# Attention and feed-forward kernel: zero matmuls counted at their cold length, and new instruction lists

## The chip, the cores and the metric

One NeuronCore of a Trainium2 chip runs the whole program. The metric is the device time of one execution in microseconds. Lower is better.

## The reference

The inputs are q, k and v of shape (8, 8, 576, 64) (batch, heads, sequence, head size) and four weight matrices; all are float32. Attention works inside chunks of 64 positions, nine to a batch entry:

```python
scores = scale * np.matmul(q_c, k_c.transpose(0, 1, 2, 4, 3))   # by chunk, scale = 1/8
scores = scores - np.max(scores, axis=-1, keepdims=True)
attn = np.exp(scores)
attn = attn / (np.sum(attn, axis=-1, keepdims=True) + 1e-09)
out = np.matmul(attn, v_c)
...
x = out.transpose(0, 2, 1, 3).reshape(4608, 512)                # heads side by side
a = x @ w1          # 512 -> 1024
b = x @ w2          # 512 -> 1024
h = a * b @ w3      # 1024 -> 1024
return h @ w_out    # 1024 -> 512, float32
```

## The kernel before

The 4608 rows are 36 groups of 128 (two chunks, eight heads). Four groups make a tile of 512 rows for the feed-forward part, so there are nine tiles. All matmuls are in bfloat16 and sum into PSUM in float32.

A group g runs through these steps; the name of each is what the lists use:

- `qk{g}.0`, `qk{g}.1`: loads of q and k, with a cast, issued by GpSimd (POOL) into `raw`. A group whose two chunks lie in two batch entries has four.
- `t{g}`: 16 or 8 transposes on TensorE into the PSUM tile `p_tr`, of which there is one. Then `kc{g}` copies k to `kT`, and `q{g}.0` and `q{g}.1` copy the two halves of q into a block diagonal tile `qd`. Each copy is on ScalarE (ACT) or VectorE (DVE). For the groups that have a `tq{g}` in SyncE's (SP) list, the transposition is a DMA into `kqT` instead, and there is no `kc`.
- `s{g}`: eight score matmuls into `p_sc`, of which there is one. `mx{g}` takes the maxima. Then `sd{g}` (subtraction, VectorE) and one wide `ex{g}` (exponential, ScalarE), or, for the groups in `EXP_8`, an `ex{g}` of eight instructions, one by head, straight from `p_sc` with no `sd`.
- `sm{g}`: sums and reciprocals. `an{g}`: the division, on VectorE or GpSimd.
- `at{g}` (four transposes on TensorE) and `ac{g}` (copy), or `ta{g}` (a DMA on SyncE's queue).
- `av{g}`: eight matmuls with v into `p_av`, and `x{g}`, the copy into the tile's x.

The weights w3 and w_out are multiplied first, by `wt` (eight transposes of a block of w3), `wc` (copy), `wm` (matmuls in four parts, `wm{block}.{part}`) and `wr` (copy). The product is `w3o`. The first two blocks of w3 come over SyncE's queue in float32 (`f0`, `f1`) and are cast by `cast0` and `cast1`. Then a tile i takes, for each of eight column blocks j, `a{i}.{j}` and `b{i}.{j}` (four matmuls each), `c{i}.{j}` (ScalarE copies a out of PSUM) and `m{i}.{j}` (VectorE multiplies it by b); and for each of four row groups `o{row}` (eight matmuls with `w3o`), `y{row}` (copy) and `z{row}` (store, SyncE). The loads `w12.{j}.{n}` bring w1 and w2 for columns j and j+1; `v{b}.{n}` bring v. `zv` and `zq` zero the tiles of v and q, `ident` makes the identity for the transposes.

Nothing is ordered at run time. `ORDER` holds one list of step names for each engine, and each engine runs its list in order: an instruction whose operands are not there holds up all behind it on its engine. `Plan.run` walks through these lists with a cost for each step. From that come the order in which the program is recorded, which buffers a step takes, and a planned start of each step. At most eight loads are under way from each of the two issuing queues.

Ahead of steps in the first 20 us of the plan, the program puts matmuls of zeros on TensorE (`fill`, line 556, tile `cold` into the PSUM tile `p_av`): so many as fit, by a formula, between the end of TensorE's step before and the planned start of the step. Line 648 gives the number:

```python
if o.engine == "PE" and o.start < WARM:
    n = int((o.start - idle_from - (2.6 if idle_from < 2 else 0.5)) / 0.217)
```

`idle_from` is 1.2 before the first step. The program built so has 26 zero matmuls: four ahead of `wt0`, ten ahead of `t0`, four ahead of `s0`, five ahead of `t2` and three ahead of `s2`.

Line numbers in the profile: 318 and 321 loads of q and k, 330 of v, 338 of w1 and w2, 347 of w3, 370 of w_out; 356 the float32 rows of w3; 392 and 397 `t`; 401 `tq`, 407 `ta`; 434 `s`; 442 `mx`; 446 `sd`; 449 and 454 `ex`; 458 and 460 `sm`; 464 `an`; 469 `at`; 480 `av`; 527 `wt`; 538 `wm`; 556 the zero matmuls; 571 `a` and `b`; 580 `m`; 600 `o`; 618 `z`; 267, 269, 271 and 273 the helper that makes all copies; 282 `zv`; 286 `zq`.

Of the kernel before, what the change touches and what calls it, by code (L numbers as in the profile page):

```python
# [22 lines left out]
WARM = 20  # L23
ORDER = {
# [14 lines left out]
           "o30 b8.4 a8.4 b8.3 a8.3 b8.5 o31 o32 o33 o34 o35a o35b ").split(),  # L39
    "ACT":  # L40
# [9 lines left out]
           "c8.0 c8.2 c8.1 c8.7 c8.6 y29 c8.5 y30 c8.4 c8.3 y35b ").split(),  # L50
    "DVE":
# [11 lines left out]
           "y25 m7.0 m7.4 m7.3 y26 x32 m7.6 m7.2 m7.1 m8.0 m8.2 m8.1 y28 m8.7 m8.6 m8.4 m8.5 m8.3 y31 y32 y33 y34 y35a ").split(),  # L63
    "POOL":
# [8 lines left out]
           "an34 an35 ").split(),  # L73
# [4 lines left out]
           "z32 z30 z33 z34 z35a z35b ").split(),  # L78
}
PACKED = (0, 1, 2, 3, 4, 5, 6, 7, 8, 9, 11, 14, 15, 16, 18, 20, 26, 28, 29, 35)  # L80
EXP_8 = (2, 9, 13, 14, 15, 31, 32)
TURN_QK = [f"tq{g}" in ORDER["SP"] for g in range(36)]
TURN_A = [f"ta{g}" in ORDER["SP"] for g in range(36)]
ROWS_F32 = sum(t[0] == "f" for t in ORDER["SP"])
# [107 lines left out]
def kernel(  # L192
# [51 lines left out]
    ident = consts.tile([P, P], bf)  # L244
# [30 lines left out]
    cold = consts.tile([P, TT], bf, name="cold")  # L275
# [30 lines left out]
    def load_qk(g):  # L306
        (b0, c0), (b1, c1) = chunks(g)
        parts = [(slice(0, P), b0, c0, 2)] if b0 == b1 else [(halves[0], b0, c0, 1), (halves[1], b1, c1, 1)]
        box = raws[g] = {"ops": []}
        packed = g in PACKED and not TURN_QK[g]  # L310
        for w, src in enumerate((q, k)):
# [65 lines left out]
    def add_group(g):  # L377
# [4 lines left out]

        turned, packed, by_head = TURN_QK[g], g in PACKED, g in EXP_8

# [262 lines left out]
    with tc.manual_schedule():  # L647
        order, spells, idle_from = plan.run(), {}, 1.2
        for o in order:
            if o.engine == "PE" and o.start < WARM:  # L650
                n = int((o.start - idle_from - (2.6 if idle_from < 2 else 0.5)) / 0.217)
                if n > 0:
                    spells[o] = n
                idle_from = o.start + o.cost
        filler = fill(spells)
        for o in order:
            for _ in range(spells.get(o, 0)):
                next(filler)
            o.emit(o.engine)
# [30 lines left out]
```

## Time and profile before

| What | us |
|---|---|
| Median of three runs | 258.38 (258.14 to 259.05) |
| The profiled execution | 258.92 |
| Its span, first to last instruction | 257.1 |
| TensorE (PE) busy | 243.6 |
| VectorE (DVE) busy | 171.5 |
| ScalarE (ACT) busy | 140.0 |
| GpSimd (POOL) busy, issuing loads included | 117.7 |

The profile is of one execution. PE is TensorE's matmuls and PEld its weight loads, which run beside them. A matmul's duration holds its drain, which overlaps the next one; how long a row of matmuls holds TensorE is read from the start of the row to the start of the next. A wait is put down to what came last by the profile.

### The profile page before, as it was taken

The page shows a single profiled execution, that of the slowest core. Times are in us where ns is not written, and L with a number is a line of the kernel's source. Part 1 is how long each engine was busy: PE and PEld are TensorE (multiplying, and loading weights), DVE is VectorE, ACT ScalarE, POOL GpSimd, SP SyncE. Part 2 cuts the span into 40 slices and gives each one's busy share as a digit, 9 for nine tenths or more (in the row PEclk, how much of TensorE's full clock was granted, in tenths as well). Part 3 has the DMA queues.
Part 4 walks back from the last instruction along what each step waited for, and adds up shares of the span by engine and source line. Part 5 has one row for each costly group of instructions (what it writes and reads, how often), then busy time and mean ns, then how long its engine had stood idle before and what let it go on. Part 6 is the DMA issues. An engine that isn't in the chain of part 4 may idle for free.

```text
span 257.1 us, 4876 instructions
## 1 busy us (share of the span) xinstructions
PE 243.6 (95%) x1850; PEld 124.1 (48%) x1850; DVE 171.5 (67%) x315; ACT 140.0 (54%) x276; POOL 117.7 (46%) x146
## 2 busy tenths in 40 slices
PE   4879999999999989999989999989999999999994
PEld 2345555555545444554544445435444544544443
DVE  3168989975599765899696368988757585332342
ACT  5449887657476658445783645453684532432200
POOL 8777558979858656088408111763131031000000
PEclk9999999999999999999999999999999999999999
DMA  8999999999999999999999938699999239400334
GB/s 200 184 197 199 169 148 147 169 167 117 133 155 157 156 157 156 157 148 150 128 146 146 115 65 162 65 144 126 220 268 253 53 116 307 174 3 0 122 119 167
DMA packets 148999, 38.33 MB, mean 149 GB/s; under 512 B 138096, under 2 KB 143472, under 8 KB 148976
## 3 DMA queue, kind: packets, MB, share of 16 engines
q0 software_dynamic: 108192, 18.88, 99.3%
q1 hardware_dynamic: 40784, 19.14, 38.4%
q8 instruction: 14, 0.23, 0.4%
q14 instruction: 9, 0.07, 0.1%
HBM read 38.80 MB, written 9.44 MB: 188 GB/s over the span
## 4 chain that ended last, share of the span: by engine, by line
PE 72%; DVE 16%; ACT 5%; DMA 5%; issue 1%; DVEq 0%; ACTq 0%
PE ffn L571 41%; PE ffn L600 17%; DMA at<-an 3%; DVE ss L458 3%; DVE qd L273 3%; PE ffn L538 3%; PE p_av L480 3%; PE p_sc L434 2%; PE p_tr L392 2%; DVE abT L580 2%; DVE nm L442 2%; PE p_av L556 2%; DVE an L464 2%; DMA stage<-in_moe_w_dram 1%; DVE sd L446 1%
## 5 line engine op out<-in xcount | busy, mean ns | idle before, releaser
L571 PE MATMUL ffn<-xt,w_sb 128*128 128x512 bf16 x576 | 135.5, 379 | 0.0
L571 PEld LDWEIGHTS <-w_sb 128*128 128x128 bf16 x576 | 53.1, 98 | 56.3
L600 PE MATMUL ffn<-w3o_sb,abT 128*128 128x512 bf16 (+1 forms) x296 | 67.2, 373 | 0.0
L271 ACT COPY a_sb<-ffn 128x512 f32<-128x512 f32 x72 | 41.4, 591 | 47.1 <-PE ffn L571 46.9
L580 DVE TENSOR_TENSOR abT<-a_sb,ffn 128x512 bf16<-128x512 f32 x72 | 47.8, 678 | 27.7 <-PE ffn L571 15.1
L464 POOL TENSOR_TENSOR an<-e,rs 128x512 bf16<-128x512 bf16 x18 | 18.9, 1049 | 79.3 <-DVE rs L460 56.9
L600 PEld LDWEIGHTS <-abT 128*128 128x128 bf16 x296 | 28.2, 98 | 30.6
L442 DVE TENSOR_REDUCE nm<-p_sc 128x8 f32<-128x512 f32 x36 | 24.5, 681 | 15.2 <-PE p_sc L434 15.1
L449 ACT ACTIVATE e<-sd 128x512 bf16<-128x512 f32 x29 | 18.3, 633 | 19.1 <-DVE sd L446 18.5
L458 DVE TENSOR_REDUCE ss<-e 128x8 f32<-128x528 bf16 x36 | 24.9, 693 | 5.0 <-ACT e L454 2.5
L318 POOL DMA_DIRECT2D raw<-in_k_dram x29 | 24.9, 867 | 4.6 <-DMA raw<-in_q_dram 2.2
L318 POOL DMA_DIRECT2D raw<-in_q_dram x29 | 25.0, 874 | 3.2 <-DMA raw<-in_k_dram 1.8
L271 ACT CAST xt<-p_av 128x512 bf16<-128x512 f32 x27 | 15.8, 586 | 16.0 <-PE p_av L480 15.8
L446 DVE TENSOR_TENSOR sd<-p_sc,nm 128x512 f32<-128x512 f32 x29 | 19.8, 683 | 0.4
L330 POOL DMA_DIRECT2D vd<-in_v_dram x16 | 18.8, 1175 | 1.5 <-DMA raw<-in_k_dram 1.0
L434 PEld LDWEIGHTS <-qd 128*128 128x128 bf16 x288 | 12.4, 98 | 12.9 <-ACT qd L271 3.4
L538 PE MATMUL ffn<-wo_sb,w3t 128*128 128x512 bf16 x64 | 17.0, 380 | 0.2 <-DVE w3t L273 0.2
L480 PEld LDWEIGHTS <-vd 128*128 128x128 bf16 x288 | 12.9, 98 | 8.1 <-DMA at<-an 1.2
L273 DVE COPY o_sb<-ffn 128x512 f32<-128x512 f32 (+1 forms) x12 | 8.0, 666 | 11.1 <-PE ffn L600 11.1
L480 PE MATMUL p_av<-at,vd 128*128 128x64 bf16 x288 | 14.3, 193 | 0.7 <-DMA at<-an 0.7
L454 ACT ACTIVATE e<-p_sc,nm 128x64 bf16<-128x64 f32 x56 | 12.3, 337 | 4.7 <-DVE nm L442 4.7
L271 ACT COPY o_sb<-ffn 128x512 f32<-128x512 f32 (+1 forms) x13 | 7.4, 572 | 11.9 <-PE ffn L600 11.8
(54 smaller groups left out, 210.2 us busy)
## 6 DMA issues: line engine op xcount, KB each, us to landing
out_dram<-o_sb SPq DMA_DIRECT2D x23, 256.0 KB, 2.3
vd<-in_v_dram POOLq DMA_DIRECT2D x16, 288.0 KB, 9.9
raw<-in_q_dram POOLq DMA_DIRECT2D x32, 128.0 KB, 8.0
raw<-in_k_dram POOLq DMA_DIRECT2D x32, 128.0 KB, 8.4
w_sb<-in_moe_w_dram POOLq DMA_DIRECT2D x16, 128.0 KB, 5.7
out_dram<-held_w SPq DMA_DIRECT2D x8, 256.0 KB, 2.6
w_sb<-in_moe_w_dram POOLq DMA_DIRECT2D x6, 256.0 KB, 7.5
stage<-in_moe_w_dram SPq DMA_DIRECT2D x2, 512.0 KB, 3.9
```

The source lines that it names most:

```text
L271: nc.scalar.copy(o, i)
L318: nc.gpsimd.dma_start(box["t"].rearrange("p (w h d) -> p w h d", w=2, h=H)[r, w], x.rearrange("h p d -> p h d"))
L330: nc.gpsimd.dma_start(vds[b % len(vds)][halves[t], :, :, t * D:(t + 1) * D].rearrange("p m c d -> p (m c) d"), v[b, NM * t:NM * (t + 1)].r ...
L442: nc.vector.tensor_reduce(nm[:, :, 0], flat(box["sc"]), axis=AX.X, op=ALU.max, negate=by_head)
L446: nc.vector.tensor_sub(sd[:], flat(box["sc"]), box["nm"].to_broadcast([P, 8, C]))
L458: nc.vector.reduce_sum(ss[:], e[:], axis=AX.X)
L464: (nc.gpsimd if eng == "POOL" else nc.vector).tensor_mul(an[:], e[:, :, :C], box["rs"].to_broadcast([P, 8, C]))
L480: nc.tensor.matmul(t[:, m, cc, :], vds[b % len(vds)][:, m, c, :], box["at"][:, 2 * cc + y, u * C:(u + 1) * C], start=True, stop=True)
L538: nc.tensor.matmul(box["wp"][:], box["t"][:, ki, :], wo_sb[:, ki, :], start=(ki == 0), stop=(ki == FO - 1))
L571: nc.tensor.matmul(t[:, :w], wt[:, ki, j * P:(j + 1) * P], x[:, ki, :], start=(ki == 0), stop=(ki == KO - 1))
L580: nc.vector.tensor_mul(box["abT"][:, j, :w], box["as", j][:, :w], box["b", j][:, :w])
L600: nc.tensor.matmul(t[:, :x1 - x0], box["abT"][:, ki, tk * P:(tk + 1) * P], w3o_sb[:, ki, x0:x1], start=(ki == 0), stop=(ki == FO - 1))
```

## The change

The formula that counts the zero matmuls is another: ahead of the first step of TensorE it takes 0.43 us for each, later 0.5 us, and it leaves 0.4 us free. All five lists are new, and so are the sets of packed groups and of groups with exponentials by head. In TensorE's list `t0` now stands first and `wt0` second. The program built so has 17 zero matmuls: thirteen ahead of `t0`, one ahead of `s0`, one ahead of `t2` and two ahead of `at0`. By the lists, 15 groups have `at` on TensorE instead of 16; 13 groups have `t` there in both. On GpSimd `qk0.0` stands ahead of `ident`.

The core of the diff: the beginnings of the lists, the parts of TensorE's that the text speaks of, the sets and the formula.

```diff
     "PE":
-          ("wt0 t0 s0 t1 wt1 t2 s1 wm0.0 s2 t3 wm0.1 wm1.0 wm1.1 wm0.2 t4 wm1.2 wm0.3 at0 wm1.3 wt2 s3 wt7 wm2.0 wm2.1 t5 "
-           "wm7.0 s4 wm2.2 wm2.3 wt4 at1 wm7.1 wm7.2 s5 wm7.3 wt5 wm4.0 wm4.1 at2 t6 wm4.2 wt6 wm4.3 wm5.0 s6 wm5.1 t7 wm6.0 "
-           "wm5.2 wm6.1 at3 av2 wm6.2 wm5.3 av0 wm6.3 wt3 av1 at4 t8 wm3.0 av3 s7 wm3.1 wm3.2 wm3.3 a0.0 a0.1 at5 b0.0 t9 "
-           "b0.1 s8 a0.4 b0.4 a0.5 at6 b0.3 a0.3 b0.5 at7 s9 av4 b0.2 av7 at8 a0.2 av5 a0.6 a0.7 b0.6 av6 t10 b0.7 a1.0 a1.4 "
...
-           "b1.5 av11 a1.6 a2.0 b1.6 b2.0 s13 a2.4 b2.5 a2.5 o4 s14 b2.4 o5 at13 s15 a2.2 a2.6 o6 a2.1 b2.2 a2.7 b2.6 s16 "
...
+          ("t0 wt0 s0 t1 wt1 wm0.0 t2 s1 at0 t3 wm1.0 wm0.1 wm0.2 s2 wm1.1 wm1.2 wt7 wm0.3 wm1.3 s3 wm7.0 t4 wm7.1 at1 wm7.2 "
+           "wt4 wm7.3 t5 wm4.0 wm4.1 s4 wt2 wm4.2 wm4.3 wt5 wm2.0 wm2.1 wm2.2 wt6 s5 wm2.3 at2 wm5.0 wm5.1 wm5.2 t6 at3 "
+           "wm5.3 wm6.0 wm6.1 av1 at4 wm6.2 s6 av2 wt3 wm6.3 av0 t7 wm3.0 av3 wm3.1 wm3.2 at5 wm3.3 a0.0 b0.0 s7 a0.1 b0.1 "
+           "t8 a0.3 a0.2 b0.2 b0.3 a0.4 b0.4 s8 t9 a0.5 a0.7 b0.5 at6 a0.6 b0.6 at7 av6 b0.7 av4 at8 s9 t10 av5 o2 av7 o1 "
...
+           "o13 s24 b4.0 b4.1 a4.3 b4.2 av20 b4.3 a4.6 a4.4 a4.7 s25 av21 o15 b4.4 a4.5 s26 b4.5 av23 b4.7 av22 b4.6 b5.0 "
+           "a5.0 a5.3 o16 s27 a5.2 o17 a5.1 s28 b5.3 a5.6 o18 s29 av24 o19 s30 b5.6 b5.2 av25 a5.5 b5.1 av26 a5.7 a5.4 b5.4 "
...
     "ACT":
-          ("cast0 zv0 wc0 kc0 q0.1 q1.0 q2.0 kc2 q2.1 ex0 wc1 ex1 kc3 q3.1 ex2 ac0 wr0 q4.1 wr1 wc7 kc5 ex3 q5.0 q5.1 ac1 "
...
+          ("zv2 zv1 cast0 kc0 cast1 wc0 q1.0 ex0 kc1 kc2 q2.1 ex1 zv0 q3.1 wr0 ex2 q4.0 wr1 q4.1 q5.0 kc5 ex3 q5.1 ex4 ex5 "
...
     "DVE":
-          ("cold zq2 zq1 zq0 cast1 q0.0 eps1 mx0 q1.1 eps0 kc1 sd0 mx1 sd1 sm0 q3.0 mx2 an0 q4.0 sm1 sm2 wc2 kc4 mx3 sd3 an1 "
...
+          ("cold zq0 zq2 zq1 q0.0 q0.1 eps1 mx0 eps0 sd0 q1.1 sm0 q2.0 mx1 wc1 q3.0 kc3 sm1 mx2 sd2 wc7 mx3 ac0 kc4 sm2 wc4 "
...
+           "q20.1 mx19 sd19 sm18 m3.3 mx20 sm19 m3.0 sm20 q21.1 x16 m3.1 mx21 m3.7 kc23 q22.0 sd21 q22.1 an20 m3.6 q23.1 "
...
+           "mx26 m4.5 m4.7 sd26 an25 m4.6 q27.0 sm26 m5.0 y16 q28.0 mx27 sd27 y17 mx28 sd28 q29.0 sm27 m5.3 mx29 q30.0 sd29 "
...
     "POOL":
-          ("ident qk0.0 qk0.1 qk1.0 qk2.0 qk1.1 wo.0 qk2.1 wo.1 qk4.0 qk4.1 qk3.0 qk3.1 wo.2 qk4.2 qk4.3 wo.3 w3.2 w3.7 "
-           "qk5.0 qk5.1 w3.4 w3.6 w3.5 qk6.0 qk6.1 qk7.0 v0.0 qk7.1 v0.1 w3.3 qk8.0 qk8.1 w12.0.0 w12.0.1 an3 w12.0.2 "
-           "w12.0.3 qk9.0 qk9.1 w12.4.0 w12.4.1 w12.4.2 w12.2.0 w12.4.3 w12.2.1 w12.2.2 w12.2.3 v1.0 v1.1 w12.6.0 w12.6.1 "
-           "w12.6.2 w12.6.3 qk10.0 qk11.0 qk10.1 an8 qk12.0 qk13.0 qk11.1 qk13.1 qk13.2 qk13.3 qk22.0 qk14.0 qk12.1 qk15.0 "
...
+          ("qk0.0 ident qk0.1 qk1.0 qk1.1 wo.0 qk2.0 qk2.1 qk3.0 wo.1 qk3.1 wo.2 w3.7 wo.3 qk4.0 qk4.1 qk4.2 an0 qk4.3 w3.4 "
+           "qk5.0 qk5.1 w3.2 w3.5 an1 w3.6 v0.0 qk6.0 qk6.1 an2 v0.1 an3 w3.3 qk7.0 qk7.1 w12.0.0 w12.0.1 w12.0.2 w12.0.3 "
+           "w12.2.0 qk8.0 qk8.1 an5 w12.2.1 w12.2.2 w12.2.3 w12.4.0 w12.4.1 w12.4.2 qk9.0 w12.4.3 w12.6.0 qk9.1 w12.6.1 "
+           "w12.6.2 w12.6.3 v1.0 v1.1 qk10.0 qk10.1 qk11.0 qk11.1 qk12.0 an7 qk12.1 qk14.0 qk13.0 qk13.1 v2.0 qk16.0 qk13.2 "
...
     "SP":
-          ("f0 f1 tq11 tq13 tq14 tq15 tq16 tq17 ta12 tq18 tq19 tq20 tq21 tq22 tq24 ta17 ta18 ta19 tq25 ta20 tq26 ta21 tq27 "
...
+          ("f0 f1 tq11 tq12 tq13 tq15 tq16 tq17 ta13 ta14 tq18 tq19 tq20 tq21 tq22 ta17 ta18 ta19 tq24 tq25 ta20 ta21 ta22 "
...
-PACKED = (0, 1, 2, 3, 4, 5, 6, 7, 8, 9, 11, 14, 15, 16, 18, 20, 26, 28, 29, 35)
-EXP_8 = (2, 9, 13, 14, 15, 31, 32)
+PACKED = (0, 1, 2, 3, 4, 5, 6, 7, 8, 9, 11, 12, 15, 16, 18, 20, 22, 24, 31, 34, 35)
+EXP_8 = (1, 4, 5, 6, 7, 10, 13, 20, 22, 25, 35)
...
-                n = int((o.start - idle_from - (2.6 if idle_from < 2 else 0.5)) / 0.217)
+                n = int((o.start - idle_from - 0.4) / (0.43 if idle_from < 2 else 0.5))
```

More of the change, by code (lines that the diff above doesn't have):

```diff
@@ L25 @@
     "PE":
[13 rows of a table removed]
-           "o30 b8.4 a8.4 b8.3 a8.3 b8.5 o31 o32 o33 o34 o35a o35b ").split(),
-    "ACT":
[9 rows of a table removed]
-           "c8.0 c8.2 c8.1 c8.7 c8.6 y29 c8.5 y30 c8.4 c8.3 y35b ").split(),
-    "DVE":
[11 rows of a table removed]
-           "y25 m7.0 m7.4 m7.3 y26 x32 m7.6 m7.2 m7.1 m8.0 m8.2 m8.1 y28 m8.7 m8.6 m8.4 m8.5 m8.3 y31 y32 y33 y34 y35a ").split(),
-    "POOL":
[8 rows of a table removed]
-           "an34 an35 ").split(),
[13 rows of a table added]
+           "b8.7 b8.3 a8.3 b8.6 b8.4 a8.6 o31 o32 o33 o34 o35a o35b ").split(),
+    "ACT":
[9 rows of a table added]
+           "y34 y35b ").split(),
+    "DVE":
[11 rows of a table added]
+           "m7.0 m7.3 sm35 m7.5 x33 m7.6 m7.4 m7.1 m7.7 m7.2 y28 m8.2 m8.0 y29 m8.1 m8.5 m8.7 m8.3 m8.4 m8.6 y33 y35a ").split(),
+    "POOL":
[8 rows of a table added]
+           "qk34.1 v7.1 an31 an33 an34 an35 ").split(),
     "SP":
[3 rows of a table removed]
-           "z32 z30 z33 z34 z35a z35b ").split(),
-}
-PACKED = (0, 1, 2, 3, 4, 5, 6, 7, 8, 9, 11, 14, 15, 16, 18, 20, 26, 28, 29, 35)
-EXP_8 = (2, 9, 13, 14, 15, 31, 32)
[3 rows of a table added]
+           "z31 z27 z32 z33 z34 z35a z35b ").split(),
+}
+PACKED = (0, 1, 2, 3, 4, 5, 6, 7, 8, 9, 11, 12, 15, 16, 18, 20, 22, 24, 31, 34, 35)
+EXP_8 = (1, 4, 5, 6, 7, 10, 13, 20, 22, 25, 35)
 TURN_QK = [f"tq{g}" in ORDER["SP"] for g in range(36)]
```

61 rows, old and new, of the table ORDER are left out of this document.

## The prediction

> **What bounds the kernel now.** I read the page first, then the busy time by stretches, then the waits of TensorE alone, then the timeline of the first 20 us, and at last single rows of groups, tiles and transfers. The page says that TensorE is nearly always busy; the stretches, of which the one from 10.34 to 20 us is left out, say where it is not. Columns after the length: busy us of PE, weight loads, VectorE, ScalarE, GpSimd, each with its instructions, then clock, DMA share, GB/s.
>
> ```profile
> PE 243.6 (95%) x1850; PEld 124.1 (48%) x1850; DVE 171.5 (67%) x315; ACT 140.0 (54%) x276; POOL 117.7 (46%) x146
> 0.00:10.34 10.34, 6.97 (x24) 2.63 (x24) 2.42 (x5) 5.54 (x5) 9.07 (x18) 1.00 1.13 193
> 20.00:44.20 24.20, 23.26 (x282) 13.92 (x281) 21.88 (x42) 20.61 (x40) 15.87 (x23) 1.00 1.52 165
> 44.20:60.00 15.80, 15.80 (x137) 8.41 (x136) 11.99 (x23) 10.44 (x24) 13.96 (x19) 1.00 1.93 162
> 60.00:120.00 60.00, 59.08 (x445) 30.75 (x443) 46.42 (x88) 35.24 (x79) 39.88 (x44) 1.00 2.02 151
> 120.00:180.00 60.00, 57.42 (x424) 28.41 (x422) 45.62 (x84) 33.19 (x61) 24.08 (x26) 1.00 1.57 121
> 180.00:253.80 73.80, 73.69 (x440) 35.60 (x437) 37.65 (x65) 29.98 (x64) 7.39 (x7) 1.00 0.63 151
> ```
>
> From 20 us to its last matmul TensorE stands idle for about 4.5 us of 233.8. So the end is set by TensorE's list of work, and by how early that list gets going: a microsecond gained at the start reaches the end, unless a load or a copy is late later on. The waits between 60 and 180 us are four, 3.4 us in all (columns: us in total, times, longest):
>
> ```profile
> PE p_sc L434 <- DVE sd L446: 1.2, 1, 1.2
> PE p_sc L434 <- ACT e L454: 0.9, 1, 0.9
> PE p_av L480 <- DMA at<-an: 0.7, 1, 0.7
> PE p_sc L434 <- ACT qd L271: 0.6, 1, 0.6
> ```
>
> The first 20 us are the other place. This is the timeline (start, duration, what, count, and in brackets the idle time before it):
>
> ```profile
> 0.73 1.28 ACT L271 ACT_TABLE_LOAD   x1 [0.73 <-PEq L674]
> 1.19 1.89 PE L556 MATMUL p_av<-cold 128*128 128x512 bf16 x4 [1.19 <-DVE cold L276]
> 2.28 0.68 POOL L321 DMA_DIRECT2D raw<-in_k_dram  x1
> 4.16 1.05 ACT L271 CAST w_sb<-stage 128x1024 bf16<-128x1024 f32 x1 [2.14 <-DMA stage<-in_moe_w_dram]
> 5.11 2.30 ACT L282 COPY vd<-cold 64x1152 f32<-64x1152 f32 x2
> 6.09 4.32 PE L556 MATMUL p_av<-cold 128*128 128x512 bf16 x10
> 10.33 0.48 PEld L392 LDWEIGHTS <-raw 128*64 128x64 bf16 x16 [0.68 <-issue]
> 10.34 0.64 PE L392 MATMUL p_tr<-ident,raw 128*64 128x128 bf16 x16
> 10.90 1.04 PE L556 MATMUL p_av<-cold 128*128 128x512 bf16 x4
> 13.32 0.64 PE L392 MATMUL p_tr<-ident,raw 128*64 128x128 bf16 x16
> 14.35 1.24 PE L556 MATMUL p_av<-cold 128*128 128x512 bf16 x5
> 16.33 0.64 PE L392 MATMUL p_tr<-ident,raw 128*64 128x128 bf16 x16 [0.74 <-DVE kT L273]
> 19.23 0.64 PE L392 MATMUL p_tr<-ident,raw 128*64 128x128 bf16 x16
> ```
>
> The ten zero matmuls before t0 (10.34) run from 6.09 to 10.34: 0.425 us each. The five at 14.35 fit into 1.24 us with a last one's drain of some 0.38, so 0.215 each. The plan counted both kinds at 0.217. What t0 needs is k of group 0; the answer on the raw tile for 1.5 to 2.5 us gives q's and k's loads from issue to landing, k's the shorter:
>
> ```profile
> DMA to landing us min/median/max: 5.6/5.7/5.8
> ```
>
> Issued at 2.28, k lands at 7.9, and the weight loads of t0 wait for nothing but "issue": the zero matmuls in front of them hold the queue for 10.34 - 7.9 = 2.4 us.
>
> **The change, part by part.**
>
> *The first string.* Thirteen zero matmuls from 1.19 at 0.425 end at 6.7, before k's landing at 7.9. wt0, which stood before t0, now stands behind it. On GpSimd q's issue moves ahead of the identity and k's stays behind both, so k's landing stays at 7.9; ScalarE's two zeroings of v and cast0, which now stand before kc0, take 2 x 2.3 + 1.05 from the end of the table load at 2.0, to 7.7, so kc0 isn't late. t0 starts at 8.0, 2.3 us earlier.
>
> *From t0 to t3.* p_tr has one buffer, so each t waits for the three copies of the one before. The chain of waits shows the first round (start, us, what):
>
> ```profile
> 10.40 0.59 PE p_tr L392 x16
> 11.01 0.59 ACT kT L271
> 11.63 0.69 DVE qd L273
> 12.35 0.59 ACT qd L271
> 12.98 0.41 PE p_sc L434 x8
> ```
>
> The rounds take 2.98, 3.01 and 2.90 us. The new lists keep three copies in a row in each round: with 2.95 a round t3 starts at 8.0 + 8.9 = 16.9. Walking the new lists by hand with these durations gives less, since q1.0, ex0 and kc1 close up: t1 10.9, t2 13.6, t3 16.1. I take 16.5 against 19.23: 2.7 us. TensorE's useful work ahead of t3 is the same in both lists but for at0 in the place of s2 (0.23 against 0.24 us), so the whole 2.7 is a lead. at0 waits for an0 on GpSimd, which comes after s0 (done at 10.9) by the five steps mx0, sd0, ex0, sm0 and an0 of at most 1.05 us each (rows below): 16.1 at the latest, before t3; queued behind at0 are t3 and the wm that follow.
>
> *The later gaps.* One, one and two zero matmuls stand where four, five and three stood. They lie in waits for copies, so that they go costs nothing as long as the clock stays up (first rival).
>
> *Who turns what.* q and k of group 12 go from TensorE to the DMA queue and those of group 14 the other way; attention of group 12 comes to TensorE and that of 13 and 14 goes. In all there are fifteen instead of sixteen `at` sets on TensorE, each of which holds it for the 0.23 us from its first row to the next:
>
> ```profile
> 23.62 0.39 PE L469 MATMUL p_at<-ident,an 128*128 128x128 bf16 x4
> 23.85 0.59 PE L538 MATMUL ffn<-wo_sb,w3t 128*128 128x512 bf16 x2
> ```
>
> Gain 0.2.
>
> *Four more groups with exponentials by head* (eleven for seven): each puts eight L454 in the place of one L449 on ScalarE and drops one L446 on VectorE.
>
> ```profile
> L446 DVE TENSOR_TENSOR sd<-p_sc,nm 128x512 f32<-128x512 f32 x29 | 19.8, 683 | 0.4
> L449 ACT ACTIVATE e<-sd 128x512 bf16<-128x512 f32 x29 | 18.3, 633 | 19.1 <-DVE sd L446 18.5 <-DVE an L464 0.4
> 22.16 1.75 ACT L454 ACTIVATE e<-p_sc,nm 128x64 bf16<-128x64 f32 x8
> ```
>
> That is 4 x (1.75 - 0.63) = 4.5 us more on ScalarE (54% busy) and 4 x 0.68 = 2.7 less on VectorE (67%): off the path. But a group by head holds p_sc for 0.68 + 1.75 instead of 1.37 us, and the next s waits for that; it is one of the four waits above. In the old list s14 to s15, both by head, are 2.8 us of matmuls apart; in the new one the closest from tile 1 on is s25 to s26 with 3.7 (a set of four wide matmuls is 0.86, an o twice that, an av 0.23). The tightest of the others is s29 to s30, 1.96 apart, in which VectorE has mx29, a copy and sd29, 1.37 without the copy. So I expect no more waiting than before.
>
> *GpSimd's queue.* Five an (0, 1, 2, 3, 5) now stand among the loads of the first tile, where one stood, and each waits there with the loads behind it. The one of before:
>
> ```profile
> 35.13 1.04 POOL L464 TENSOR_TENSOR an<-e,rs 128x512 bf16<-128x512 bf16 x1 [4.63 <-DVE rs L460]
> 46.76 2.48 POOL L338 DMA_DIRECT2D w_sb<-in_moe_w_dram  x4
> 57.31 1.03 PE L571 MATMUL ffn<-xt,w_sb 128*128 128x512 bf16 x4
> DMA to landing us min/median/max: 8.3/8.3/8.3
> GB/s 165 162 160 158 197 181 197 200 179 186 182 178 179 191 190 190 142 67 38 12 72 164 123 199 129 83 143 149 163 130 127 157 117 142 167 164 154 157 161 160
> ```
>
> It stood 4.63 us, and the transfers ran dry behind it: the last row is 30 to 45 us in 40 parts, down to 12 GB/s near 37. Five an at 1.04 are 5.2 us, about what wait and an took (5.7). They stand behind loads enough that their sums should be ready when GpSimd comes by, and loads are landed six or more us after issue, which hides a stall of 1 to 2 us. The lead needs this: the last weights of columns 6 and 7, issued at 48.6, land at 56.9 (8.3), and a0.6 uses them at 57.3. In the new list they go ahead of v1's two loads, and the dry spell may go; so I take that they come earlier by at least the lead.
>
> *The rest of the lists* is dealt anew. No row shows it. Its bounds: the four waits go (-3.4) or come twice (+3.4). I take 0, nearest to the waits that are there, since the mix of work per tile is the same.
>
> Sum: -2.7 - 0.2 = -2.9. The profiled execution took 258.92 with a span of 257.1, so 1.8 lie around it; it stands 0.5 above the median of 258.38. The changed kernel's span is 254.2, its median 255.5.
>
> **The rivals.**
>
> *The clock falls back.* For: between the end of the string (6.7) and s0 (10.6) there are only t0, wt0 and one zero matmul, 1.25 us of work in 3.9; after that a round has about 1.5 of 2.95. In the trace the first four zero matmuls did not bring the spacing of 0.215, nor did the ten before 10.3, over 4 us after they began. The clock column says 1.00 all along, so only the spacing tells. Against: from 10.34 to 16.33 there was a hole of 1.0 us (11.9 to 13.0) and the spacing held. Price: t0, t1, t2 take 0.57 more each and s0 0.25, 2.0 by t3, and what lies between t1 and t2 overruns by 0.3; then up to 4.2 us of dense work at half speed, as long as the ten took, cost 2.1. So 2.3 to 4.4, 257.8 to 259.9; I take 259.5, since the rounds stay thin until t3. It decides if t0's sixteen take 1.1 us.
> The Trainium skill, "TensorE: Matmul & The Clock Gate", Part 1, has the array at half clock by default, released after a free-running window of about 3.4 us with work and throttled after an idle one; Part 4 adds that transposes do not count as work there in the same way. By Part 4 the stretch from 6.7 to 10.6 is idle and this rival would be the likelier; the trace of before does not decide it, as there are zero matmuls on both sides of its transposes.
>
> *The loads don't follow.* If the five an stall the stream as the one did, TensorE comes 2.7 early to weights that had 0.4 to spare: 2.3 of the lead is lost, 257.8. For: each an waits for a chain on two engines. Against: places and sizes above.
>
> *The late waits double:* 255.5 + 3.4 = 258.9; s29 to s30 and VectorE's heavier tile 0 (31 of its entries from m0.0 to m1.0, 19 before) speak for it.
>
> *The string was no hindrance:* t0 starts near 10 all the same, 258.2. The "issue" row and the landing speak against it.
>
> **How the numbers follow.** Forecast 66%, clock 13%, loads 8%, late waits 10%, no hindrance 3%. About 0.3% (0.8 us) is what a measurement can tell from no change. Faster: forecast and half of the loads' case, 70%. Same: the other half, 4% of the late waits, 2% of the clock, the last case, 13%. Slower: 11% of the clock and 6% of the late waits, 17%. Range: below, t3 at 16.1 and half of the four waits gone, 258.4 - 3.1 - 0.2 - 1.9 = 253.2; above, 259.0, which takes in the late waits and the lower part of the clock's case.
>
> **What would show it.** t0 near 8.0 with sixteen in 0.6 us, t3 near 16.5, the first L571 2.7 us earlier, no an that waits over 2 us among the first tile's loads, no wait at L571 before 60 us, idle time of TensorE after 60 us near 3.4. Wrong: spacing of 0.1 us in t0; a wait for w_sb or raw; more than 4 us of waits at p_sc.

## The result, and the profile after

| | before | after |
|---|---|---|
| Median of 20 runs, us | 258.15 (255.95 to 259.09) | 254.16 (252.91 to 256.43) |
| Ratio, 95% interval | 1 | 0.9859 (0.9834 to 0.9884) |
| Profiled execution, us | 258.92 | 253.89 |
| Its span, us | 257.1 | 252.1 |

The changed kernel is 1.4% faster, 4.0 us by the medians, where 2.9 were forecast. 254.16 lies in the range; the sign and the first mechanism were right, and the size was short by 1.1 us. The two profiled executions differ by more, 5.0 us: that of the kernel before took 0.8 us more than its median, that of the changed kernel 0.3 less. What the traces add up to is to be held against 5.0.

The timeline of TensorE after, first 20 us (start, duration, what, count, idle time before it):

```profile
1.19 5.63 PE L556 MATMUL p_av<-cold 128*128 128x512 bf16 x13 [1.19 <-DVE cold L276]
7.01 0.64 PE L392 MATMUL p_tr<-ident,raw 128*64 128x128 bf16 x16 [0.19 <-DMA raw<-in_k_dram]
7.79 0.62 PE L527 MATMUL ffn<-ident,w_sb 128*128 128x128 bf16 x8
8.25 0.38 PE L556 MATMUL p_av<-cold 128*128 128x512 bf16 x1
9.75 0.41 PE L434 MATMUL p_sc<-kT,qd 128*128 128x64 bf16 x8 [1.12 <-DVE qd L273]
10.09 0.64 PE L392 MATMUL p_tr<-ident,raw 128*64 128x128 bf16 x16
13.01 0.64 PE L392 MATMUL p_tr<-ident,raw 128*64 128x128 bf16 x16 [1.08 <-ACT kT L271]
15.65 0.64 PE L392 MATMUL p_tr<-ident,raw 128*64 128x128 bf16 x16 [0.28 <-ACT qd L271]
```

t0 waits for k's load and no longer for the zero matmuls: 7.01 instead of 10.34. Then 10.09, 13.01 and 15.65 instead of 13.32, 16.33 and 19.23. The first wide matmul (L571) starts at 39.23, in the kernel before at 44.21 (the first row is of the changed kernel, the second of the one before):

```profile
39.23 1.03 PE L571 MATMUL ffn<-xt,w_sb 128*128 128x512 bf16 x4
44.21 1.03 PE L571 MATMUL ffn<-xt,w_sb 128*128 128x512 bf16 x4
```

From the first start of an L571 to the last start, both kernels take about 200.4 us, so the 5.0 us are there before the first tile begins, and nothing is won or lost behind it on balance. The rows give the first and the last start, before and after; the trace of the changed kernel lacks 19 of the 576 records:

```profile
L571 PE MATMUL ffn<-xt,w_sb x576: 376/379/389, 44.2 to 244.7; 128*128 128x512 bf16 x192
L571 PE MATMUL ffn<-xt,w_sb x557: 376/379/389, 39.2 to 239.7; 128*128 128x512 bf16 x186
```

The waits of TensorE in the changed kernel from 17 to 60 us, then from 60 to 180 us (us in total, times, longest):

```profile
PE p_av L480 <- DMA vd<-in_v_dram: 1.0, 1, 1.0
PE ffn L538 <- issue: 0.3, 2, 0.2
PE ffn L538 <- DMA wo_sb<-in_moe_w_out_dram: 0.3, 1, 0.3
...
PE p_sc L434 <- DVE qd L273: 0.8, 1, 0.8
PE p_sc L434 <- issue: 0.5, 1, 0.5
```

After 60 us there are 1.3 us of waits where 3.4 were, but two of the rows above are new in kind: v of batch 1 lands too late for av6 (1.0 us, before 60 us), and s11 waits for a copy of q (0.8 us). The chain of waits around s11 (start, us, what) says what stands behind that copy:

```profile
51.33 7.59 DMA raw<-in_k_dram
58.99 8.72 DMA kqT<-raw
68.06 0.40 DVE at L273
68.48 0.55 DVE qd L273
69.07 0.41 PE p_sc L434 x8
```

The load of group 11, its transposition by DMA, the copies, s11: TensorE, now earlier, has run into the loads. (Rows of the chain under 0.2 us are left out.)

### The profile page after: what moved, and what is told of

Its sections match the earlier page's. It is cut to its first block, busy times and chain, and to the rows that moved or that the text cites. A ratio compares the mean times of both kernels' runs of the same rounds, so it can differ in the third digit from the quotient of the medians.

```text
span 252.1 us, 4848 instructions
## 1 busy us (share of the span) xinstructions
PE 239.1 (95%) x1804; PEld 122.9 (49%) x1837; DVE 167.8 (67%) x313; ACT 139.5 (55%) x296; POOL 122.8 (49%) x151
## 4 chain that ended last, share of the span: by engine, by line
PE 68%; DMA 6%; DVE 3%; issue 1%; another core or an unknown queue 1%; ACT 1%; DVEq 0%; ACTq 0%; SPq 0%
PE ffn L571 40%; PE ffn L600 22%; DMA kqT<-raw 3%; DMA raw<-in_k_dram 3%; PE p_sc L434 2%; PE p_av L480 2%; PE p_at L469 1%; DVE abT L580 1%; DVE nm L442 0%; DVE ss L458 0%; DVE an L464 0%; DVE qd L273 0%; ACT a_sb L271 0%; PE p_tr L397 0%
## 5 line engine op out<-in xcount | busy, mean ns | idle before, releaser
L571 PE MATMUL ffn<-xt,w_sb 128*128 128x512 bf16 x557 | 133.0, 379 | 1.0
L571 PEld LDWEIGHTS <-w_sb 128*128 128x128 bf16 x576 | 53.2, 98 | 57.2 <-issue 0.8
L600 PE MATMUL ffn<-w3o_sb,abT 128*128 128x512 bf16 (+1 forms) x288 | 66.0, 373 | 0.5
L464 POOL TENSOR_TENSOR an<-e,rs 128x512 bf16<-128x512 bf16 x23 | 24.8, 1080 | 80.0 <-DVE rs L460 31.8
L271 ACT CAST xt<-p_av 128x512 bf16<-128x512 f32 x29 | 17.0, 585 | 23.6 <-PE p_av L480 23.5
L449 ACT ACTIVATE e<-sd 128x512 bf16<-128x512 f32 x25 | 15.8, 630 | 14.4 <-DVE sd L446 14.1
L454 ACT ACTIVATE e<-p_sc,nm 128x64 bf16<-128x64 f32 x88 | 19.1, 328 | 6.5 <-DVE nm L442 6.4
L446 DVE TENSOR_TENSOR sd<-p_sc,nm 128x512 f32<-128x512 f32 x25 | 17.0, 681 | 0.3
L538 PE MATMUL ffn<-wo_sb,w3t 128*128 128x512 bf16 x58 | 15.8, 379 | 1.1 <-issue 0.3
L271 ACT COPY o_sb<-ffn 128x512 f32<-128x512 f32 (+1 forms) x17 | 9.6, 579 | 8.6 <-PE ffn L600 5.6
L273 DVE COPY o_sb<-ffn 128x512 f32<-128x512 f32 (+1 forms) x8 | 5.3, 657 | 12.5 <-PE ffn L600 12.5
```

The costliest lines, as they stand in the source:

```text
L271: nc.scalar.copy(o, i)
L454: nc.scalar.activation(e[:, i, :C], x[:, i, :], ACT.Exp, bias=box["nm"][:, i, :])
L464: (nc.gpsimd if eng == "POOL" else nc.vector).tensor_mul(an[:], e[:, :, :C], box["rs"].to_broadcast([P, 8, C]))
L571: nc.tensor.matmul(t[:, :w], wt[:, ki, j * P:(j + 1) * P], x[:, ki, :], start=(ki == 0), stop=(ki == KO - 1))
L600: nc.tensor.matmul(t[:, :x1 - x0], box["abT"][:, ki, tk * P:(tk + 1) * P], w3o_sb[:, ki, x0:x1], start=(ki == 0), stop=(ki == FO - 1))
```

## The experiments

**The count alone, and the lists alone.** The first has the lists of before and the new formula, the second the new lists and the old formula.

```diff
-                n = int((o.start - idle_from - (2.6 if idle_from < 2 else 0.5)) / 0.217)
+                n = int((o.start - idle_from - 0.4) / (0.43 if idle_from < 2 else 0.5))
```

> The lists of before with the new count alone: 7 zero matmuls ahead of wt0, 4 ahead of t0, then 2, 2 and 1. Theory (the string held t0 and the lead reaches the end): wt0 stays at 5.3, t0 starts at 8.0 when k has landed, 2.3 us earlier than in the kernel before, and the time falls by about as much, to 256.0. Rival (the lists bring the gain): t0 is earlier but what follows waits on, 257.5 or more.

> The new lists with the old count: 16 zero matmuls ahead of t0, then 2, 3 and 5. Theory: the string ends between 7.3 (fast spacing from 6.6) and 8.0, against k's landing at 6.9, so t0 is 0.4 to 1.0 later than in the changed kernel and the time is 254.6 to 255.2; nearly all of the gain is in the lists, which have t0 first. Rival (clock): with more zero matmuls the fast spacing holds in more executions, and the median is 253.5 or less.

The count alone: 256.05, ratio 0.9922 (0.9898 to 0.9946). t0 starts at 8.03, as expected, and the lead reaches the end. Its timeline also shows what the broken string costs: t0 itself is slow, as are the two zero matmuls behind it.

```profile
5.35 1.03 PE L527 MATMUL ffn<-ident,w_sb 128*128 128x128 bf16 x8 [0.99 <-ACT w_sb L271]
8.03 1.06 PE L392 MATMUL p_tr<-ident,raw 128*64 128x128 bf16 x16
9.02 1.03 PE L556 MATMUL p_av<-cold 128*128 128x512 bf16 x2
```

The lists alone: 254.60, ratio 0.9868 (0.9834 to 0.9903), as expected and not to be told from the changed kernel. So the two parts don't add up: on the old lists the count is worth 2.1 us, on the new ones nothing that these runs can tell. The new lists have t0 behind one string that starts at 1.19 and is over when k lands or before, with thirteen zero matmuls (row above) or, here, with sixteen:

```profile
1.19 5.32 PE L556 MATMUL p_av<-cold 128*128 128x512 bf16 x16 [1.19 <-DVE cold L276]
7.29 0.64 PE L392 MATMUL p_tr<-ident,raw 128*64 128x128 bf16 x16 [0.78 <-DMA raw<-in_k_dram]
```

**t0 first on the old lists.**

```diff
-          ("wt0 t0 s0 t1 wt1 t2 s1 wm0.0 s2 t3 wm0.1 wm1.0 wm1.1 wm0.2 t4 wm1.2 wm0.3 at0 wm1.3 wt2 s3 wt7 wm2.0 wm2.1 t5 "
+          ("t0 wt0 s0 t1 wt1 t2 s1 wm0.0 s2 t3 wm0.1 wm1.0 wm1.1 wm0.2 t4 wm1.2 wm0.3 at0 wm1.3 wt2 s3 wt7 wm2.0 wm2.1 t5 "
-          ("cast0 zv0 wc0 kc0 q0.1 q1.0 q2.0 kc2 q2.1 ex0 wc1 ...
+          ("cast0 zv0 kc0 q0.1 wc0 q1.0 q2.0 kc2 q2.1 ex0 wc1 ...
```

(with the new count)

> The lists of before with the new count, and t0 ahead of wt0, kc0 and q0.1 ahead of wc0: 14 zero matmuls in one string, then 1, 2, 1. Theory (t0 first gives one string without a break, the fast spacing comes by 6.7 and t0 itself is fast): t0 starts at 7.4 and takes 0.6 us instead of 8.0 and 1.0 in the version with the new count alone, s0 is 1.0 to 1.2 earlier, and the time is 255.0 against 256.05 there; what is left to the changed kernel, 0.9, is the rest of the lists. Rival (the rest of the lists has the difference): 256.0.

255.76, ratio 0.9914 (0.9888 to 0.9941): by the interval the same as the count alone. t0 is fast, but it starts at 7.93 and not at 7.4, since k lands only at 7.8; s0 is 0.5 earlier (10.58 against 11.10) instead of 1.0 to 1.2, and 0.3 is left in the median. The expected 255.0 was missed. The changed kernel is 1.6 us ahead. This version keeps the waits of the kernel before from 60 us on:

```profile
PE p_sc L434 <- ACT e L454: 1.3, 1, 1.3
PE p_sc L434 <- DVE sd L446: 1.2, 1, 1.2
PE p_sc L434 <- ACT qd L271: 0.6, 1, 0.6
```

These 3.1 us are three of the four waits there; the new lists have 1.3 us. But they do not explain the 1.6: from the first L571 to the last this version takes 200.2 us, no more than the changed kernel, whose waits for the loads weigh as much. What puts its profiled execution behind lies ahead of the first tile: its first L571 starts at 41.81, 2.6 us later, of which 0.6 is work that the new lists have behind it; its t0 starts 0.9 later.

**The identity first again.**

```diff
-          ("qk0.0 ident qk0.1 qk1.0 ...
+          ("ident qk0.0 qk0.1 qk1.0 ...
```

> The changed kernel with the identity ahead of q's load of group 0 on GpSimd, as before (14 zero matmuls in the first string, then 1, 1, 1). Theory (the place of the first load sets when all the first loads land): q and k land at 7.2 and 7.9 as in the kernel before, t0 starts at 8.0, 1.0 later, and the time is 255.1. Rival (the landing differs from one execution to the next): k lands near 6.9, t0 at 7.2 at the end of the string, 254.3.

255.73, ratio 0.9913 (0.9883 to 0.9943). k landed at 7.4, between the two theories, and t0 started at 7.57. That is half a microsecond of the 1.6 by which it stands above the changed kernel; much of the rest goes with another thing. Eight of its ten executions had a mean clock of 0.993 and took 256.1 on average, the two at full clock 254.9 and 253.8. The stretches of the profiled one show what that is (length, busy us of PE, weight loads, VectorE, ScalarE, GpSimd, then the granted clock):

```profile
9.50:12.90 3.40, 2.12 (x34) 1.53 (x36) 2.95 (x9) 2.41 (x4) 1.80 (x4) 1.00 1.58 184
12.90:16.30 3.40, 1.69 (x33) 1.22 (x34) 2.35 (x5) 1.87 (x4) 3.17 (x5) 1.00 1.33 202
16.30:19.70 3.40, 3.18 (x21) 1.59 (x22) 2.53 (x5) 3.39 (x10) 1.38 (x2) 0.50 1.45 193
19.70:23.00 3.30, 3.18 (x35) 1.85 (x33) 2.50 (x4) 2.07 (x4) 3.17 (x5) 1.00 1.44 194
```

Behind a stretch with 1.69 us of work the clock is halved for 3.4 us, just when the dense `wm` begin; the first wide matmul comes at 40.92. This is the first rival of the prediction, in the changed kernel too: six of its 20 executions had 0.986 to 0.993, and they took 255.5 on average, the other fourteen 254.0. It is not all of the spread: one of the six took 253.87, and one of the fourteen 256.43.

**No zero matmuls, the string alone, more zero matmuls.**

```diff
-WARM = 20
+WARM = 0
```

> The changed kernel without any zero matmul. Clock theory: t0 starts at 7.0 but its sixteen transposes take 1.1 us, the slow spacing lasts until TensorE is dense at 16 to 20 us, and the time is 2.3 to 4.4 above the changed kernel: 256.5 to 258.6. Rival (the spacing early on does not matter, since the copies set the rounds): 254.2.

254.14 (four runs), ratio 0.9881 (0.9827 to 0.9934). The rival's number, but not for its reason. The spacing is slow until 16 us, as the clock theory had it:

```profile
7.33 1.07 PE L392 MATMUL p_tr<-ident,raw 128*64 128x128 bf16 x16 [7.33 <-DMA raw<-in_k_dram]
14.14 1.06 PE L392 MATMUL p_tr<-ident,raw 128*64 128x128 bf16 x16 [0.64 <-ACT kT L271]
17.21 0.64 PE L392 MATMUL p_tr<-ident,raw 128*64 128x128 bf16 x16 [0.91 <-ACT qd L271]
```

The first wide matmul comes at 40.32, 1.1 later than in the changed kernel, and yet the last one starts 0.7 earlier: v is there when TensorE comes, and the wait for group 11 is 0.2 instead of 0.8. That lead was being spent on waiting. So with the new lists the zero matmuls bring nothing that the medians show: 254.14 without, 254.16 with them. The old lists were not run without them.

Two versions of the formula follow, each in the place of the first line; the comments are added here:

```diff
-... / (0.43 if idle_from < 2 else 0.5))
+... / (0.43 if idle_from < 2 else 50))      # the string alone
+... / (0.43 if idle_from < 2 else 0.22))    # more: 13, then 3, 4, 5
```

> The changed kernel with the string of thirteen zero matmuls alone, none in the later gaps. Clock theory (a window of 3.4 us with too little on TensorE drops the clock for the next window, and the zero matmuls in the gaps keep it above): more executions at 0.993 or 0.986 than the 6 of 20 of the changed kernel, most of them, and a median near 255.4. Rival (transposes and score matmuls alone keep it up): 6 of 20 again and 254.2.

> The changed kernel with the later gaps counted at 0.22 us instead of 0.5: 13 zero matmuls, then 3, 4 and 5 instead of 1, 1 and 2. They fit into the waits for copies, so nothing is held up. Clock theory (the executions of the changed kernel with a mean clock of 0.993 fell back for one window of 3.4 us around 13 to 20 us, since TensorE was too idle in the window before; the slow third of its executions are these): no execution at 0.993, the slow ones near 255.5 to 256 go, the median is 253.7. Rival (those executions are slow for another reason): a median of 254.2 and as many above 255.4.

The string alone: four of six at 0.993 or less, as the theory said, but a median of 253.43 (253.0 to 256.2; ratio 0.9839, 0.9791 to 0.9886), not 255.4: two of the four took 253.1 and 253.8, two 255.6 and 256.2. More zero matmuls: none of six at 0.993, none above 254.9, and still a median of 254.18 (0.9845, 0.9819 to 0.9871) instead of 253.7. The fallback of the clock goes and the executions above 255 with it, but in the profiled execution TensorE then waits at s11 for longer:

```profile
PE p_sc L434 <- DVE qd L273: 2.0, 1, 2.0
```

**The loads.** First an3 leaves GpSimd's queue, then group 11 is loaded ahead of group 10.

```diff
-... v0.1 an3 w3.3 qk7.0 ...            (GpSimd)
+... v0.1 w3.3 qk7.0 ...
-... mx4 wc2 sm3 wr4 ...                (VectorE)
+... mx4 wc2 sm3 an3 wr4 ...
```

> The changed kernel with an3 on VectorE, behind sm3, instead of on GpSimd among the loads. Load theory (the loads set the end of the changed kernel: GpSimd stands 1.4 us and more for an3, so that the loads up to those of group 11 come later, and s11 waits for their transposition by DMA): the weights of columns 6 and 7, v of batch 1 and the loads of group 11 land 1.5 to 2.4 us earlier, the waits for v and at s11 go, and the time falls by 1.0 to 2.0, to 252.2 to 253.2. Rival (the copies set it): VectorE has 0.68 us more to do near 27 us, the waits stay, and the time is 254.2 or more.

```diff
-... v1.0 v1.1 qk10.0 qk10.1 qk11.0 qk11.1 qk12.0 ...    (GpSimd)
+... v1.0 v1.1 qk11.0 qk11.1 qk10.0 qk10.1 qk12.0 ...
-... at8 s9 t10 av5 o2 av7 o1 ...                        (TensorE)
+... at8 s9 av5 o2 av7 t10 o1 ...
-... m0.7 q10.0 mx9 q10.1 kc10 sd9 sm9 ...               (VectorE)
+... m0.7 mx9 sd9 q10.0 q10.1 kc10 sm9 ...
```

> The changed kernel with the loads of group 11 ahead of those of group 10, t10 moved behind av7, and mx9 and sd9 ahead of the copies of group 10. Load theory (everything behind s11 follows the landing of the transposition of group 11): it is issued and lands 1.9 us earlier, s11 doesn't wait, t10 waits for at most 0.5, and the time falls by 0.5 to 1.2, to 253.0 to 253.7. Rival (the transposition by DMA takes as long as the loads around it last, whenever it is issued): it lands less than 0.7 earlier and the time stays at 254.2.

With an3 on VectorE the transposition of group 11 lands at 66.5 instead of 67.7, both new waits are gone, and the profiled execution took 252.50; but the median stays at 254.19 (0.986, 0.9816 to 0.9904), as three of six executions had the clock at 0.993 or less. Partly as expected, and by itself undecided.

Group 11 first: 252.41, with all five runs between 251.98 and 252.65, ratio 0.9777 (0.9752 to 0.9803). More than expected. Its transposition is issued at 56.8 and lands in 6.8 us where it took 8.7, and s11 follows without a wait (these two rows are of its timeline):

```profile
67.09 1.03 PE L571 MATMUL ffn<-xt,w_sb 128*128 128x512 bf16 x4
67.95 0.40 PE L434 MATMUL p_sc<-kqT,qd 128*128 128x64 bf16 x8
```

Nothing but these orders differs from the changed kernel. But they are orders on three engines, and the loads were not moved alone. That the loads are the cause rests on two versions more: with an3 on VectorE and without zero matmuls the waits for them go or shrink as well, by other edits, and these take 198.6 us from the first L571 to the last, group 11 first 198.9, the changed kernel 200.4. The difference is about the 1.8 us of the two waits. So the loads did set its end.

**Together.** Group 11 first with the denser zero matmuls, and with an3 on VectorE besides:

> The version with group 11 first (252.41) and the denser later zero matmuls (13, 3, 4, 5) together. Theory (with the wait for group 11 gone, the time is again TensorE's list from the first wide matmul on, and the only loss left in the first 20 us is the fallback of the clock): no execution at a clock of 0.993, a median of 251.9 to 252.4. Rival (the time is now set elsewhere): no less than 252.4, whatever the clock.

> The same with an3 on VectorE as well. Theory of the loads: they no longer set the end, so their coming 1 to 2 us earlier brings nothing, and VectorE's extra 0.68 us costs at most 0.5: 251.9 to 252.9. Rival (v of batch 1 still holds av6 or the like): 251.5 or less.

252.49 (0.9771, 0.9735 to 0.9806) and 252.80 (0.9790, 0.9756 to 0.9823). Neither is told from group 11 alone, which is 2.2% faster than the kernel before. The first missed what was expected, if narrowly: one execution of six at 0.993 was left, and the time lies 0.1 above the expected 251.9 to 252.4, on the side of the rival. The second came out as expected, within 251.9 to 252.9. What sets the time of these versions was not followed.

## Why the prediction was right, and where it was short

*The first string.* Right: t0 waited for zero matmuls at their slow length. The count alone, on the old lists, took 2.1 us off the time, where 2.3 was forecast for the start of t0. What was mis-sized is k's landing, taken at 7.9: it came at 6.87, since its load took 4.2 us and not 5.6.

```profile
DMA to landing us min/median/max: 4.2/4.2/4.2
```

In the thirteen profiled executions here k landed at 6.9 to 7.2 with q's load first (nine, k issued at 2.6) and at 7.35 to 7.9 with the identity first (four, k issued at 2.3). So the order that the prediction passed over as neutral brings k in earlier by about half a microsecond; why a load issued later lands earlier was not settled.

*From t0 to t3.* 3.6 us (15.65 for 19.23) instead of 2.7. t0 starts 1.0 earlier than forecast, at 7.01 and not at 8.0, so the landing makes all of the difference. The rounds of 3.08, 2.92 and 2.64 us are 8.6 in all, 0.1 more than the 8.5 that the forecast had between its walk by hand (2.9, 2.7, 2.5) and its mean of 2.95.

*The lead reaches the end.* It did, but not by the reason given. The first wide matmul is 5.0 us earlier; about 0.6 of this is a t and an s that stand behind it now, less an at that stands ahead of it. So between t3 and there the lead grew from 3.6 to 4.4 like for like; the 0.8 was not followed. Behind it 1.8 us went into the waits for v and for group 11, and about as much came back from the old waits that are gone. That the two cancel is luck: neither was in the sum. More lead would not have helped, as the version without zero matmuls shows, which comes to the first wide matmul 1.1 later and takes the same time.

*The loads don't follow.* The place was named wrongly. None of the five an on GpSimd stalled it for over 1.4 us (two of them):

```profile
25.02 1.09 POOL L464 TENSOR_TENSOR an<-e,rs 128x512 bf16<-128x512 bf16 x1
28.59 1.04 POOL L464 TENSOR_TENSOR an<-e,rs 128x512 bf16<-128x512 bf16 x1 [1.38 <-ACT e L454]
```

and no w1 or w2 was late. But that v1 had been put behind those weights, and that group 11 has a load, a DMA transposition and two copies ahead of s11, was not followed past a0.6. That is the step that failed: the slack was worked out for one user of the stream and not for the next ones, and it cost 1.8 us.

*The rest of the lists.* Taken at 0. The four waits of 3.4 us after 60 us became two of 1.3, of which 0.8 is the new one for group 11; with the 1.0 for v before 60 us, 2.3 us of waits stand where 3.4 stood: the waits did not double, as the third rival had it. The version with t0 first on the old lists is 1.6 us of median behind the changed kernel, but its t0 also starts 0.9 later, as k lands later. If the old lists pass on all of that, 0.7 is left to the other lists, if nothing, 1.6: an estimate from these two versions. With the landing of k this makes up the shortfall of 1.1; how much each has of the median was not separated.

*The clock.* It fell in six of 20 executions, which took 1.4 us more on average, so it is part of the result and not a rival to it; the price was put at 2.3 to 4.4. That was too high: a slow stretch between 10 and 16 us can lie in waits for copies. In the profiled execution of group 11 first the clock is halved from 10.2 to 13.6, and it took 252.62, where the four at full clock took 251.98 to 252.65. Between 16 and 20 us, where the matmuls are dense, it costs more: in the string alone the profiled execution with the fall from 15.95 to 19.36 took 255.56, the two without a fall of 3.4 us 253.0. Two more of its executions with a low clock took only 253.1 and 253.8; where their clock fell is not on record. The test named in the prediction, sixteen transposes in 1.1 us, was too narrow: the fall came after t0.

The rule of the Trainium skill ("TensorE: Matmul & The Clock Gate", Part 1) that a free-running window of about 3.4 us with work releases the clock, and one without it throttles, agrees: the halved stretches are 3.4 us long. An idle window was not needed, 1.7 us of work were too little.

That transposes do not count (Part 4 of that page of the Trainium skill) does not agree where the clock has to rise. Without zero matmuls it rose behind a stretch of 3.4 us with 2.76 us of work, of which 1.24 were not transposes (a wide matmul of 0.63 and a score row of 0.61; the row is in the last section). With more zero matmuls, a stretch with 2.35 us of zero matmuls alone did not raise it, and the string stayed slow to its end near 6.9:

```profile
0.13:3.54 3.41, 2.35 (x6) 0.89 (x7) 1.73 (x4) 2.78 (x3) 2.43 (x9) 1.00 0.51 159
```

So transposes count, unless zero matmuls count for less than other matmuls, which no run separates. Whether they count against a fall, these traces do not decide. The stretch before the fall above had 1.69 us, and 0.6 without its transposes; the one of the changed kernel from 6.58 to 10.00 kept the clock and had more by both counts, 1.96 and 0.87 (the end of the string 0.24, a zero matmul 0.38, the begun score row 0.25):

```profile
6.58:10.00 3.42, 1.96 (x34) 1.26 (x33) 1.48 (x4) 3.40 (x5) 3.42 (x6) 1.00 1.48 165
```

*Slips in the working.* Half of the four waits is 1.7 us and not 1.9, so the lower end of the range is 253.4 by its own terms. Between 30 and 45 us the loads of the kernel before landed 5.4 to 6.5 us after their issue (medians by kind), not six or more. And s34 and s35, with two sets of wide matmuls between them (1.73), stand closer than s29 and s30. None of the three changes what came out.

## What to carry to other kernels

Where one engine is busy nearly all the time, a start that comes earlier is worth its length only as far as the next late load: work out the slack for every user of the load stream behind the step that moves, not for the first. Filler work, as the zero matmuls are, must be counted at the length that it has when it runs: counted at half of it, it held up t0 by 2.4 us. Whether it is needed at all is worth a run of its own; with the new lists the kernel without it was as fast. A change that frees a microsecond may show nothing (more zero matmuls here) until the wait that takes it up is removed as well.

## What the runs showed of the hardware that was not expected

In the three profiles that show a fall, the clock of TensorE fell for 3.4 us behind windows of 3.4 us with 1.5 to 1.7 us of work: 1.53 in the string alone (12.54 to 15.95), 1.61 in group 11 first (6.77 to 10.18), 1.69 above. The busy time alone is no bound: in the version with t0 first on the old lists it held behind a window with 1.56, all of it zero matmuls:

```profile
4.39:7.80 3.41, 1.56 (x7) 0.49 (x5) 0.69 (x1) 2.82 (x3) 3.41 (x5) 1.00 1.57 178
```

In the version without zero matmuls the clock was slow through a window with 2.26 and rose behind one with 2.76:

```profile
9.30:12.70 3.40, 2.26 (x32) 1.94 (x32) 2.65 (x8) 2.13 (x4) 2.72 (x5) 1.00 1.55 178
12.70:16.10 3.40, 2.76 (x33) 2.06 (x31) 1.84 (x4) 1.73 (x4) 2.08 (x3) 1.00 1.34 202
```

The clock column says 1.00 in that slow time before the first rise: it shows later falls, not the slow start. And a DMA transposition of the same size took 8.7 us from issue to landing in the changed kernel and 6.8 when its loads came before those of group 10; what makes the difference was not tried.
